# Batch 1 back on TensorE transposes, later work on the DMA crossbar, and new scheduler durations: one change to a fused attention and maxout kernel

## Chip, cores, metric

One core of one Trainium2 chip. The metric is device time in microseconds (us) of one execution. A kernel is timed several times; medians are quoted, over all runs. Ratios are of fast runs alone (here: a run is slow when it is over 1.5% above the fastest of the same kernel). Each run also has a mean granted TensorE clock. Within a call of experiments all kernels run on the same chip, beside runs of the kernel before.

## The reference

Attention over 4 batches, 8 heads, 768 positions, head size 64, with a full causal mask for some heads and "first 4 keys plus a window of 64" for the others, then a feed-forward layer:

```python
scores = scale * np.matmul(q, k.transpose(0, 1, 3, 2))      # masked, softmax over keys
attn   = np.matmul(a, v)                                     # 4 x 8 x 768 x 64
x      = attn.transpose(0, 2, 1, 3).reshape(3072, 512)
out    = np.maximum(x @ w1, x @ w2) @ w_out                  # w1, w2: 512x1024, w_out: 1024x512
```

The kernel uses max(a, b) = b + relu(a - b): out = x (w2 w_out) + relu(x (w1 - w2)) w_out. So it prepares `wd = w1 - w2` and `wm = w2 w_out` once. "Dense work" below means the products with `wd`, `wm` and `w_out`.

## The kernel before

The program is not a loop nest. It is a list of operations with durations, dependences and priorities; a list scheduler in the kernel file runs through them once, at build, on a model clock, and emits each in the order in which the model started it. Each engine, and the SP queue that issues DMAs, then keeps that fixed order on the chip, waiting wherever the chip is later than the model was: in the timeline that the prediction shows, TensorE stands 2.44 us before a score matmul with dense matmuls next in its list.

```python
FIRST_QK_DMA = 4      # from this pair of heads on: q, k narrow and by crossbar
FIRST_X_DMA = 8       # from this pair on: attention output by crossbar
LAT = {"PE": 0.25, "DVE": 0.15, "ACT": 0.2, "POOL": 0.2, "DMA": 1.8}
...
# load of q, k or v of pair i (two heads of one batch, 384 KB of float32)
ld_ops[tag, i] = P.add({"DMA": 1.15 if wide else 1.75}, fn, ...)
...
# q and k of a pair, after the cast to bf16: crossbar ...
if i >= FIRST_QK_DMA:
    tops.append(P.add({"DMA": 0.9}, move, deps=[casts[which]], ...))      # dma_start_transpose
    continue
# ... or six TensorE transposes into PSUM and an eviction
t = P.add({"PE": 0.34}, tr, ...)
tops.append(P.add({"DVE": 1.02, "ACT": 1.02}, evac, deps=[t], ...))       # (cut)
# the scores of a pair depend on both
op = P.add({"PE": cost}, go, deps=tops, row=True, prio=(0, i, bt[0]), ...)
...
if FIRST_X_DMA <= i < len(pairs) - 1:
    xt_ops[b, hp] = P.add({"DMA": 0.9}, xmove, deps=norms, ...)           # crossbar
else:
    t = P.add({"PE": 0.34}, xtr, ...)                                     # TensorE
...
# dense work: four matmuls a piece, lower priority than attention
t = P.add({"PE": PIECE * GT / 2400.0 + 0.005}, up, deps=... wd_ops + [xt_ops[b, hp] ...], prio=(4, b, g, 0, f))
...
P.add({"DMA": 0.8}, store, deps=[e], ...)
```

There are 16 pairs; pairs 4 to 7 are batch 1. All DMAs of q, k, v, weights, output and all crossbar transposes go through the SP queue, in order.

Terms: the crossbar is the DMA path that transposes on the way (`dma_start_transpose`). A wide load of q or k fetches rows of 512 B, a narrow one of 256 B. An eviction is the copy of a result out of PSUM. qt, kt and xt are the transposed q, k and attention output; a wait on kt is TensorE standing before a score matmul until the transposed k has landed. A block is six TensorE transposes. Half clock means a granted TensorE clock of about 0.50.

The softmax here doesn't subtract the row's maximum and nothing guards it: scores larger than these inputs give would overflow.

Of the kernel before, what the change touches and what calls it, by code (L numbers as in the profile page):

```python
# [13 lines left out]
NEG = -30000.0  # L14
ACT_SLACK = 0.6
PIECE = 4
FIRST_QK_DMA = 4
FIRST_X_DMA = 8


SWITCH = 0.1
# [112 lines left out]
def kernel(  # L134
# [13 lines left out]
    nc = tc.nc  # L148
# [9 lines left out]
    d_model = H * D  # L158
    d_ff = moe_w1.shape[1]
    KC = d_model // 128  # L160
    FC = d_ff // 128
    HP = H // 2
# [15 lines left out]
    w1_f = consts.tile([128, KC, d_ff], F32)  # L178
    w2_f = consts.tile([128, KC, d_ff], F32)
# [25 lines left out]
    P = Planner(res)  # L205
# [69 lines left out]
    def plan_load(i, b, hp, which):  # L275
        src = (q, k, v)[which][b, 2 * hp:2 * hp + 2]
        tag = ("ldq", "ldk", "ldv")[which]
        wide = which < 2 and i < FIRST_QK_DMA
        pat = ("h (m p r) d -> p h m (r d)", dict(p=128, r=2)) if wide else ("h (n p) d -> p h n d", dict(p=128))

        def fn(eng):
            dst = P[tag, i]
            if which < 2 and not wide:
                dst = dst.rearrange("p h m (r d) -> p h (m r) d", d=D)
            nc.sync.dma_start(out=dst, in_=src.rearrange(pat[0], **pat[1]))  # L285
        ld_ops[tag, i] = P.add({"DMA": 1.15 if wide else 1.75}, fn, acq=[(tag, (tag, i))], prio=(len(ld_ops),))

    def plan_weight(name, arr, dst, parts):
        src = arr.rearrange("(c p) f -> p c f", p=128)
        w = src.shape[1] // parts  # L290
        for i in range(parts):
            def fn(eng, i=i):
                nc.sync.dma_start(out=dst[:, i * w:(i + 1) * w, :], in_=src[:, i * w:(i + 1) * w, :])
            ld_ops[name, i] = P.add({"DMA": 6.0 / parts}, fn, prio=(len(ld_ops),))


    xt_ops = {}
# [3 lines left out]
    def plan_pair(i, b, hp):  # L301
# [15 lines left out]
        for which in range(2):  # L317
            tb, tt = (("qb", "qt"), ("kb", "kt"))[which]

            if i >= FIRST_QK_DMA:  # L320
                def move(eng, tb=tb, tt=tt):
                    nc.sync.dma_start_transpose(
                        out=P[tt, i].rearrange("p (n c) -> p n c", c=128),
                        in_=P[tb, i].rearrange("p n h d -> p (n h d)"))
                tops.append(P.add({"DMA": 0.9}, move, deps=[casts[which]], acq=[(tt, (tt, i))], rel=[(tb, i)],
                                  prio=(0, i, which)))
                continue

            def tr(eng, which=which, tb=tb):
                src = P[tb, i]  # L330
                o = P["mmT", i, which].bitcast(BF16)
                for n in range(NB):
                    nc.tensor.transpose(o[:, n * 128:(n + 1) * 128], src[:, n].rearrange("p h d -> p (h d)"), ident)

            def evac(eng, which=which, tt=tt):
                o, in_ = P[tt, i], P["mmT", i, which].bitcast(BF16)[:, 0:S]
                if i < FIRST_QK_DMA:
                    o = o.rearrange("q (m p r) -> q m r p", p=128, r=2)
                    in_ = in_.rearrange("q (m r p) -> q m r p", p=128, r=2)
                ev(eng)(out=o, in_=in_)  # L340
            t = P.add({"PE": 0.34}, tr, deps=[casts[which], ident_op], acq=[("mm", ("mmT", i, which)), (tt, (tt, i))],
                      rel=[(tb, i)], prio=(1, i, which))
            tops.append(P.add({"DVE": 0.56, "ACT": 0.72} if i >= FIRST_QK_DMA else {"DVE": 1.02, "ACT": 1.02}, evac, deps=[t],
                              rel=[("mmT", i, which)], prio=(1, i, which)))
# [111 lines left out]
                out=P["xt", b][:, hp, :].rearrange("p (n c) -> p n c", c=128),  # L456
                in_=P["x", i].rearrange("p n c -> p (n c)"))
        if FIRST_X_DMA <= i < len(pairs) - 1:
            xt_ops[b, hp] = P.add({"DMA": 0.9}, xmove, deps=norms, prio=(0, i, NS),
                                  use=[("x", ("x", i), 3), ("xt", ("xt", b), XT_USES)])  # L460
        else:
            t = P.add({"PE": 0.34}, xtr, deps=norms, acq=[("mm", ("mmX", i))], prio=(2, i, NS),
                      use=[("x", ("x", i), 3), ("xt", ("xt", b), XT_USES)])
            xt_ops[b, hp] = P.add({"DVE": 0.56, "ACT": 0.72}, xev, deps=[t], rel=[("mmX", i)], prio=(0, i, NS))
# [4 lines left out]
    def plan_weights_prep():  # L469
        w2_ops = []  # L470
        for c in range(KC):
            w2_ops.append(P.add({"POOL": 1.15, "ACT": 0.95, "DVE": 0.75}, copy(w2_bf[:, c, :], w2_f[:, c, :]),
                                deps=[ld_ops["w2", c // 2]], prio=(3, 0, c)))
        for c in range(0, FC, 2):
            wo_ops.append(P.add({"POOL": 1.15, "ACT": 0.95, "DVE": 0.75}, copy(wo_bf[:, c:c + 2, :], wo_f[:, c:c + 2, :]),
                                deps=[ld_ops["wo", c // 4]], prio=(3, 1, c)))
        for c in range(KC):
            def fn(eng, c=c):
                nc.vector.tensor_sub(out=wd_bf[:, c, :], in0=w1_f[:, c, :], in1=w2_bf[:, c, :])
            wd_ops.append(P.add({"DVE": 1.15}, fn, deps=[ld_ops["w1", c // 2], w2_ops[c]], prio=(3, 2, c)))  # L480
        t_ops = []
        for f in range(FC):
            def tr(eng, f=f):
                psb = P["mmW", f].bitcast(BF16)
                for c in range(KC):
                    nc.tensor.transpose(psb[:, c * 128:(c + 1) * 128], w2_bf[:, c, f * 128:(f + 1) * 128], ident)

            def evac(eng, f=f):
                ev(eng)(out=w2t[:, f, :], in_=P["mmW", f].bitcast(BF16)[:, 0:d_model])
            t = P.add({"PE": 0.22}, tr, deps=w2_ops, acq=[("mm", ("mmW", f))], prio=(3, 0, f))  # L490
            t_ops.append(P.add({"DVE": 0.42, "ACT": 0.5}, evac, deps=[t], rel=[("mmW", f)], prio=(2, 0, f)))
        for c in range(KC):
            def mm(eng, c=c):
                for f in range(FC):
                    nc.tensor.matmul(P["mmM", c], lhsT=w2t[:, f, c * 128:(c + 1) * 128], rhs=wo_bf[:, f, :],  # L495
                                     start=(f == 0), stop=(f == FC - 1))

            def evac(eng, c=c):
                ev(eng)(out=wm_bf[:, c, :], in_=P["mmM", c])
            t = P.add({"PE": FC * 0.2165}, mm, deps=t_ops + wo_ops, acq=[("mm", ("mmM", c))], prio=(3, 1, c))  # L500
            wm_ops.append(P.add({"DVE": 0.6, "ACT": 0.6}, evac, deps=[t], rel=[("mmM", c)], prio=(2, 1, c)))


    def plan_dense(b):
        mm = "mm" if b < B - 1 else "sc"
        prev = [None]
        for g in range(NG):
            ups = []
            for f in range(FC):
                t = None  # L510
                for part in range(KC // PIECE):
                    def up(eng, g=g, f=f, part=part):
                        for c in range(part * PIECE, (part + 1) * PIECE):
                            nc.tensor.matmul(P["mmH", b, g, f][:, 0:GT], lhsT=wd_bf[:, c, f * 128:(f + 1) * 128],  # L514
                                             rhs=P["xt", b][:, c, g * GT:(g + 1) * GT],
                                             start=(c == 0), stop=(c == KC - 1))
                    t = P.add({"PE": PIECE * GT / 2400.0 + 0.005}, up,
                              deps=[t] if part else wd_ops + [xt_ops[b, hp] for hp in range(HP)] + [prev[0]],
                              acq=[] if part else [(mm, ("mmH", b, g, f))],
                              use=[("xt", ("xt", b), XT_USES)] + ([] if part else [("gt", ("gt", b, g), GT_USES)]),  # L520
                              prio=(3, b, g, 0, f) if part else (4, b, g, 0, f))
# [10 lines left out]
            for t in range(GT // 128):  # L532
# [22 lines left out]
                def store(eng, g=g, t=t, c0=c0):  # L555
# [1 line left out]
                    nc.sync.dma_start(out=out[r0:r0 + 128, :], in_=P["ot", b, g, t])  # L557
                e = P.add({"ACT": 0.6, "DVE": 0.6}, evac, deps=[last], acq=[("ot", ("ot", b, g, t))],
                          rel=[("mmY", b, g, t)], prio=(0, 0, 9))
                P.add({"DMA": 0.8}, store, deps=[e], rel=[("ot", b, g, t)], prio=(0, 0, 9))  # L560

    pairs = [(b, hp) for b in range(B) for hp in range(HP)]

# [2 lines left out]
    with tc.manual_schedule():  # L566
# [3 lines left out]
        for h in range(H):  # L570
            def fn(eng, h=h):
                nc.vector.tensor_scalar(out=msk[:, h], in0=code, scalar1=thr[:, h:h + 1], scalar2=None, op0=ALU.is_ge)
            mask_ops.append(P.add({"DVE": 0.35}, fn, prio=(1, h // 2, 3)))
        for i in (0, 1):
            for w in range(3):
                plan_load(i, *pairs[i], w)
        plan_weight("w2", moe_w2, w2_f, 2)
        for i in (2, 3):
            for w in range(3):
                plan_load(i, *pairs[i], w)  # L580
        plan_weight("wo", moe_w_out, wo_f, 2)
        plan_weight("w1", moe_w1, w1_f, 2)
        for i in range(HP, len(pairs)):
            for w in range(3):
                plan_load(i, *pairs[i], w)
# [46 lines left out]
```

## Time and profile before

| | before |
|---|---|
| timed runs | 213.3 us median (211.2 to 215.2) |
| span of the profiled run | 208.5 us |
| TensorE busy / idle in the span | 183.5 / 25.0 us |
| of the idle: first 47 us / 47 to 150 us | 13.9 / 7.2 us |
| waits of the scores for k, after 47 us | 7.0 us in 6 waits |
| DMA packets | 98,916 |

Read it from TensorE: idle time at the start is in good part the fill of the pipeline (the longest wait, 6.9 us, is for the first q); idle time later is what better order could remove. The lines are in the prediction.

### The profile page before, as it was taken

To read this page: it belongs to the slowest core of one execution; us is meant where nothing else is said; L and a number is where in the kernel's file an instruction comes from. 1 tells how busy PE (TensorE), PEld (TensorE's weight loads), DVE (VectorE), ACT (ScalarE), POOL (GpSimd) and SP (SyncE) were. 2 spreads that over 40 slices of the span, in tenths; PEclk is the share of its full clock that TensorE was granted. 3 is DMA by queue.
4 is the path that set the end of the run, shared out by engine and by line. 5 is a ranking of instruction groups with operands and counts; after the bars stand their busy time and mean duration, and the time that the engine had idled before them with its cause. 6 is when DMAs were issued, how large, how long until landed. Compare 5 with 4: busy or idle time off the path is not lost.

```text
span 208.5 us, 4406 instructions
## 1 busy us (share of the span) xinstructions
PE 183.5 (88%) x1702; PEld 95.2 (46%) x1702; DVE 119.5 (57%) x273; ACT 124.0 (59%) x240; POOL 47.6 (23%) x59
## 2 busy tenths in 40 slices
PE   0388886999999799959997999979999999999992
PEld 0244553544554356523463545534454465444540
DVE  7799989957796477614574357427454084030700
ACT  2489699724888788947866795959692200212021
POOL 0155547053333132331231332314000000000000
PEclk9999999999999999988999999999999999999999
DMA  4999999969999999999999999999630210212112
GB/s 117 268 344 323 258 350 410 250 129 220 236 174 240 176 246 218 173 195 191 233 175 207 229 251 205 228 171 252 156 27 15 89 50 0 101 53 101 50 50 101
DMA packets 98916, 37.84 MB, mean 181 GB/s; under 512 B 87632, under 2 KB 93776, under 8 KB 98896
## 3 DMA queue, kind: packets, MB, share of 16 engines
q1 hardware_dynamic: 98752, 37.56, 87.1%
q8 instruction: 13, 0.21, 0.5%
q14 instruction: 7, 0.06, 0.1%
q10 hardware_dynamic: 144, 0.01, 0.0%
HBM read 25.17 MB, written 6.29 MB: 151 GB/s over the span
## 4 chain that ended last, share of the span: by engine, by line
PE 42%; DMA 26%; DVE 13%; SPq 6%; ACT 5%; issue 3%; POOL 2%; POOLq 0%; ACTq 0%; DVEq 0%
PE bank_80 L543 8%; DMA vn_87<-in_v_dram 6%; DMA kn_86<-in_k_dram 6%; SPq L285 4%; PE bank_79 L543 4%; PE bank_79 L514 4%; DMA kt_100<-kb_93 3%; PE bank_80 L514 3%; DMA kn_84<-in_k_dram 3%; DMA vn_89<-in_v_dram 3%; PE bank_80 L495 3%; DMA out_dram<-ot_125 3%; PE bank_74 L543 2%; PE bank_73 L543 2%; DMA kn_85<-in_k_dram 2%
## 5 line engine op out<-in xcount | busy, mean ns | idle before, releaser
L514 PEld LDWEIGHTS <-wd_bf 128*128 128x128 bf16 x256 | 23.0, 98 | 16.6 <-issue 3.0
L368 ACT ACTIVATE at_101<-bank_73 128x512 bf16<-128x512 f32 x16 | 9.6, 597 | 12.4 <-PE bank_74 L356 12.4
L379 DVE TENSOR_TENSOR at_101<-at_101,msk 128x512 bf16<-128x512 bf16 x16 | 8.0, 500 | 12.0 <-ACT at_101 L368 12.0
L356 PE MATMUL bank_73<-qt_98,kt_100 64*128 64x256 bf16 (+1 forms) x48 | 9.2, 271 | 5.9 <-DMA kt_100<-kb_93 5.9
L356 PEld LDWEIGHTS <-kt_100 64*128 64x128 bf16 x160 | 5.6, 94 | 17.1 <-issue 8.5
L543 PEld LDWEIGHTS <-gt_124 128*128 128x128 bf16 x96 | 8.9, 100 | 9.9 <-issue 1.4
L543 PEld LDWEIGHTS <-gt_123 128*128 128x128 bf16 x96 | 8.6, 98 | 9.8 <-issue 0.8
L379 DVE TENSOR_TENSOR at_109<-at_109,msk 128x384 bf16<-128x384 bf16 x16 | 7.9, 493 | 8.9 <-ACT at_109 L368 8.8
L368 ACT ACTIVATE at_107<-bank_75,bias_j 128x512 bf16<-128x512 f32 x16 | 11.1, 695 | 2.4 <-PE bank_76 L356 2.3
L356 PEld LDWEIGHTS <-kt_99 64*128 64x128 bf16 x160 | 5.5, 95 | 13.2 <-issue 8.7
L368 ACT ACTIVATE at_103<-bank_75,bias_64 128x512 bf16<-128x512 f32 x16 | 11.1, 692 | 0.6 <-PE bank_76 L356 0.6
L356 PE MATMUL bank_73<-qt_97,kt_99 64*128 64x256 bf16 (+1 forms) x48 | 9.5, 276 | 2.2 <-DVE kt_99 L340 1.1
L527 DVE TENSOR_SCALAR gt_124<-bank_80 128x384 bf16<-128x384 f32 x9 | 5.0, 558 | 10.8 <-ACT ot_127 L553 5.8
L368 ACT ACTIVATE at_104<-bank_76,bias_64 128x512 bf16<-128x512 f32 x16 | 11.1, 696 | 0.0
L368 ACT ACTIVATE at_108<-bank_76,bias_j 128x512 bf16<-128x512 f32 x16 | 11.1, 691 | 0.0
L368 ACT ACTIVATE at_111<-bank_75,bias_j 128x256 bf16<-128x256 f32 x16 | 7.7, 480 | 5.2 <-PE bank_76 L356 5.2
L368 ACT ACTIVATE at_105<-bank_73 128x512 bf16<-128x512 f32 x16 | 9.8, 613 | 1.6 <-PE bank_74 L356 1.6
L543 PE MATMUL bank_79<-wo_bf,gt_124 128*128 128x512 bf16 x40 | 10.1, 379 | 0.0
L553 ACT COPY ot_125<-bank_80 128x512 f32<-128x512 f32 x3 | 1.8, 585 | 14.0 <-PE bank_80 L543 14.0
L379 DVE TENSOR_TENSOR at_105<-at_105,msk 128x512 bf16<-128x512 bf16 x16 | 8.0, 502 | 3.6 <-ACT at_105 L368 3.6
L543 PE MATMUL bank_80<-wo_bf,gt_123 128*128 128x512 bf16 x40 | 10.0, 380 | 0.0
L368 ACT ACTIVATE at_106<-bank_74 128x512 bf16<-128x512 f32 x16 | 9.9, 621 | 0.0
(225 smaller groups left out, 494.8 us busy)
## 6 DMA issues: line engine op xcount, KB each, us to landing
w_f<-in_moe_w_dram SPq DMA_DIRECT2D x4, 1024.0 KB, 9.2
qn_81<-in_q_dram SPq DMA_DIRECT2D x6, 384.0 KB, 4.7
kn_84<-in_k_dram SPq DMA_DIRECT2D x6, 384.0 KB, 5.6
vn_87<-in_v_dram SPq DMA_DIRECT2D x6, 384.0 KB, 6.5
wo_f<-in_moe_w_out_dram SPq DMA_DIRECT2D x2, 1024.0 KB, 8.2
out_dram<-ot_125 SPq DMA_DIRECT2D x8, 256.0 KB, 2.3
out_dram<-ot_126 SPq DMA_DIRECT2D x8, 256.0 KB, 2.4
out_dram<-ot_127 SPq DMA_DIRECT2D x8, 256.0 KB, 2.4
```

Of the source, the lines that this page charges most:

```text
L285: nc.sync.dma_start(out=dst, in_=src.rearrange(pat[0], **pat[1]))
L356: nc.tensor.matmul(P["sc", i, st, hh][:, off:off + w], lhsT=kt[64 * hh:64 * hh + 64, j * 128:(j + 1) * 128], rhs=qt[64 * hh:64 * hh + 64, ...
L368: nc.scalar.activation(out=P["at", i, st, hh][:, 0:n], in_=P["sc", i, st, hh][:, 0:n], func=ACT.Exp, scale=scale, bias=bias)
L379: nc.vector.tensor_mul(out=at[:, 0:n], in0=at[:, 0:n], in1=mk)
L495: nc.tensor.matmul(P["mmM", c], lhsT=w2t[:, f, c * 128:(c + 1) * 128], rhs=wo_bf[:, f, :], start=(f == 0), stop=(f == FC - 1))
L514: nc.tensor.matmul(P["mmH", b, g, f][:, 0:GT], lhsT=wd_bf[:, c, f * 128:(f + 1) * 128], rhs=P["xt", b][:, c, g * GT:(g + 1) * GT], start=( ...
L527: nc.vector.tensor_relu(out=o, in_=i_)
L543: nc.tensor.matmul(ps, lhsT=lhsT, rhs=rhs, start=(i == 0), stop=(i == KC + FC - 1))
L553: ev(eng)(out=P["ot", b, g, t], in_=P["mmY", b, g, t])
```

## The change

Its intent: batch 1 keeps wide loads and TensorE transposes for q, k; the crossbar serves q, k of batches 2 and 3 and the attention output from batch 1; w1 comes in column halves, so that dense work can start on half of it. Beside that, the scheduler's durations for DMAs are changed, and the weight product is cut in pairs of matmuls. Core of the diff:

```diff
-FIRST_QK_DMA = 4
-FIRST_X_DMA = 8
+FIRST_QK_DMA = 8
+FIRST_X_DMA = 4
-        ld_ops[tag, i] = P.add({"DMA": 1.15 if wide else 1.75}, fn, ...)
+        ld_ops[tag, i] = P.add({"DMA": 1.15 if wide else 1.85}, fn, ...)
-                tops.append(P.add({"DMA": 0.9}, move, ...))
+                tops.append(P.add({"DMA": 1.35}, move, ...))
-                    o = o.rearrange("q (m p r) -> q m r p", p=128, r=2)
-                    in_ = in_.rearrange("q (m r p) -> q m r p", p=128, r=2)
+                    o = o.rearrange("q (m p r) -> q m p r", p=128, r=2)
+                    in_ = in_.rearrange("q (m r p) -> q m p r", p=128, r=2)
-            xt_ops[b, hp] = P.add({"DMA": 0.9}, xmove, ...)
+            xt_ops[b, hp] = P.add({"DMA": 1.35}, xmove, ...)
-                P.add({"DMA": 0.8}, store, ...)
+                P.add({"DMA": 0.75}, store, ...)
 # (cut) weights: w1 loaded in column halves, wd = w1 - w2 in eight halves of high priority
-            wd_ops.append(P.add({"DVE": 1.15}, fn, deps=[ld_ops["w1", c // 2], w2_ops[c]], prio=(3, 2, c)))
+                wd_ops.append(P.add({"DVE": 0.6}, fn, deps=[ld_ops["w1", c, half * FC // 2], w2_ops[c]],
+                                    prio=(0.5, 2, c)))
-            t = P.add({"PE": FC * 0.2165}, mm, deps=t_ops + wo_ops, acq=[("mm", ("mmM", c))], prio=(3, 1, c))
+            for f0 in range(0, FC, 2):          # (cut) two matmuls a piece
+                t = P.add({"PE": 2 * 0.2165}, mm, ..., prio=(5, 0, c) if f0 == 0 else (3.5, 0, c))
-                              deps=[t] if part else wd_ops + [xt_ops[b, hp] for hp in range(HP)] + [prev[0]],
+                              deps=[t] if part else wd_ops[KC * (f // (FC // 2)):][:KC] + [xt_ops[b, hp] for hp in range(HP)] + [prev[0]],
```

More of the change, by code (lines that the diff above doesn't have):

```diff
@@ L285, in fn, with plan_weight @@
             nc.sync.dma_start(out=dst, in_=src.rearrange(pat[0], **pat[1]))
-        ld_ops[tag, i] = P.add({"DMA": 1.15 if wide else 1.75}, fn, acq=[(tag, (tag, i))], prio=(len(ld_ops),))
-    def plan_weight(name, arr, dst, parts):
-        src = arr.rearrange("(c p) f -> p c f", p=128)
-        w = src.shape[1] // parts
-        for i in range(parts):
-            def fn(eng, i=i):
-                nc.sync.dma_start(out=dst[:, i * w:(i + 1) * w, :], in_=src[:, i * w:(i + 1) * w, :])
-            ld_ops[name, i] = P.add({"DMA": 6.0 / parts}, fn, prio=(len(ld_ops),))
+        ld_ops[tag, i] = P.add({"DMA": 1.15 if wide else 1.85}, fn, acq=[(tag, (tag, i))], prio=(len(ld_ops),))
+    def plan_weight(name, arr, dst, rows, cols):
+        src = arr.rearrange("(c p) f -> p c f", p=128)[:, rows, cols]
+        mb = 512e-6 * (rows.stop - rows.start) * (cols.stop - cols.start)
+        def fn(eng):
+            nc.sync.dma_start(out=dst[:, rows, cols], in_=src)
+        op = P.add({"DMA": mb * 2.8}, fn, prio=(len(ld_ops),))
+        for c in range(rows.start, rows.stop):
+            for f in range(cols.start // 128, cols.stop // 128):
+                ld_ops[name, c, f] = op
     xt_ops = {}
@@ L324, in move @@
                         in_=P[tb, i].rearrange("p n h d -> p (n h d)"))
-                tops.append(P.add({"DMA": 0.9}, move, deps=[casts[which]], acq=[(tt, (tt, i))], rel=[(tb, i)],
+                tops.append(P.add({"DMA": 1.35}, move, deps=[casts[which]], acq=[(tt, (tt, i))], rel=[(tb, i)],
                                   prio=(0, i, which)))
@@ L458, in plan_pair @@
         if FIRST_X_DMA <= i < len(pairs) - 1:
-            xt_ops[b, hp] = P.add({"DMA": 0.9}, xmove, deps=norms, prio=(0, i, NS),
+            xt_ops[b, hp] = P.add({"DMA": 1.35}, xmove, deps=norms, prio=(0, i, NS),
                                   use=[("x", ("x", i), 3), ("xt", ("xt", b), XT_USES)])
@@ L472, in plan_weights_prep, with fn @@
             w2_ops.append(P.add({"POOL": 1.15, "ACT": 0.95, "DVE": 0.75}, copy(w2_bf[:, c, :], w2_f[:, c, :]),
-                                deps=[ld_ops["w2", c // 2]], prio=(3, 0, c)))
+                                deps=[ld_ops["w2", c, f] for f in range(FC)], prio=(3, 0, c)))
         for c in range(0, FC, 2):
             wo_ops.append(P.add({"POOL": 1.15, "ACT": 0.95, "DVE": 0.75}, copy(wo_bf[:, c:c + 2, :], wo_f[:, c:c + 2, :]),
-                                deps=[ld_ops["wo", c // 4]], prio=(3, 1, c)))
-        for c in range(KC):
-            def fn(eng, c=c):
-                nc.vector.tensor_sub(out=wd_bf[:, c, :], in0=w1_f[:, c, :], in1=w2_bf[:, c, :])
-            wd_ops.append(P.add({"DVE": 1.15}, fn, deps=[ld_ops["w1", c // 2], w2_ops[c]], prio=(3, 2, c)))
+                                deps=[ld_ops["wo", c_, f] for c_ in (c, c + 1) for f in range(KC)], prio=(3, 1, c)))
+        for half in range(2):
+            fs = slice(half * d_ff // 2, (half + 1) * d_ff // 2)
+            for c in range(KC):
+                def fn(eng, c=c, fs=fs):
+                    nc.vector.tensor_sub(out=wd_bf[:, c, fs], in0=w1_f[:, c, fs], in1=w2_bf[:, c, fs])
+                wd_ops.append(P.add({"DVE": 0.6}, fn, deps=[ld_ops["w1", c, half * FC // 2], w2_ops[c]],
+                                    prio=(0.5, 2, c)))
         t_ops = []
@@ L492, in plan_weights_prep, with mm @@
         for c in range(KC):
-            def mm(eng, c=c):
-                for f in range(FC):
-                    nc.tensor.matmul(P["mmM", c], lhsT=w2t[:, f, c * 128:(c + 1) * 128], rhs=wo_bf[:, f, :],
-                                     start=(f == 0), stop=(f == FC - 1))
+            t = None
+            for f0 in range(0, FC, 2):
+                def mm(eng, c=c, f0=f0):
+                    for f in range(f0, f0 + 2):
+                        nc.tensor.matmul(P["mmM", c], lhsT=w2t[:, f, c * 128:(c + 1) * 128], rhs=wo_bf[:, f, :],
+                                         start=(f == 0), stop=(f == FC - 1))
+                t = P.add({"PE": 2 * 0.2165}, mm, deps=[t] + (t_ops + wo_ops if not f0 else []),
+                          acq=[] if f0 else [("mm", ("mmM", c))], prio=(5, 0, c) if f0 == 0 else (3.5, 0, c))
             def evac(eng, c=c):
                 ev(eng)(out=wm_bf[:, c, :], in_=P["mmM", c])
-            t = P.add({"PE": FC * 0.2165}, mm, deps=t_ops + wo_ops, acq=[("mm", ("mmM", c))], prio=(3, 1, c))
             wm_ops.append(P.add({"DVE": 0.6, "ACT": 0.6}, evac, deps=[t], rel=[("mmM", c)], prio=(2, 1, c)))
@@ L559, in plan_dense @@
                           rel=[("mmY", b, g, t)], prio=(0, 0, 9))
-                P.add({"DMA": 0.8}, store, deps=[e], rel=[("ot", b, g, t)], prio=(0, 0, 9))
+                P.add({"DMA": 0.75}, store, deps=[e], rel=[("ot", b, g, t)], prio=(0, 0, 9))
     pairs = [(b, hp) for b in range(B) for hp in range(HP)]
@@ L573 @@
             mask_ops.append(P.add({"DVE": 0.35}, fn, prio=(1, h // 2, 3)))
-        for i in (0, 1):
-            for w in range(3):
-                plan_load(i, *pairs[i], w)
-        plan_weight("w2", moe_w2, w2_f, 2)
-        for i in (2, 3):
-            for w in range(3):
-                plan_load(i, *pairs[i], w)
-        plan_weight("wo", moe_w_out, wo_f, 2)
-        plan_weight("w1", moe_w1, w1_f, 2)
+        ORDER = ("p0", "p1", "w2", "p2", "p3", "wo", "w1")
+        for what in ORDER:
+            if what[0] == "p":
+                for w in range(3):
+                    plan_load(int(what[1:]), *pairs[int(what[1:])], w)
+            elif what == "w2":
+                for c in (0, 2):
+                    plan_weight("w2", moe_w2, w2_f, slice(c, c + 2), slice(0, d_ff))
+            elif what == "wo":
+                for c in (0, 4):
+                    plan_weight("wo", moe_w_out, wo_f, slice(c, c + 4), slice(0, d_model))
+            else:
+                for half in (0, 1):
+                    plan_weight("w1", moe_w1, w1_f, slice(0, KC), slice(half * d_ff // 2, (half + 1) * d_ff // 2))
         for i in range(HP, len(pairs)):
```

## The prediction

> **What bounds the kernel now.** I read the page first (engine shares and the 40 slices), then busy time by stretches, then TensorE's waits after 47 us, then the order of time around its longest wait, then the groups of the lines that the change touches.
>
> ```profile
> PE 183.5 (88%) x1702; PEld 95.2 (46%) x1702; DVE 119.5 (57%) x273; ACT 124.0 (59%) x240; POOL 47.6 (23%) x59
> PE   0388886999999799959997999979999999999992
> PEclk9999999999999999988999999999999999999999
> DMA  4999999969999999999999999999630210212112
> ```
>
> TensorE (PE) is the busiest engine. Its row shows two regions: the first ten slices (to about 50 us) with holes, and then nearly solid 9s to the end with four thin slices (7, 5, 7, 7). The DMA row is full until about 150 us and then nearly empty. So two things could set the end: TensorE work, or the DMA stream that feeds attention until 150 us. Busy time by stretches (columns: stretch, its length, then busy us and instruction counts of PE, PEld, DVE, ACT, POOL, the granted clock, DMA share, GB/s):
>
> ```profile
> 38.00:47.00 9.00, 8.55 (x69) 4.23 (x66) 6.35 (x11) 4.19 (x9) 3.29 (x3) 1.00 0.89 168
> 47.00:60.00 13.00, 12.87 (x118) 6.25 (x117) 9.72 (x19) 9.68 (x20) 4.14 (x5) 1.00 1.36 213
> 60.00:75.00 15.00, 13.53 (x160) 6.97 (x158) 8.58 (x20) 11.53 (x24) 3.82 (x5) 1.00 1.15 206
> 75.00:82.00 7.00, 7.00 (x84) 3.90 (x82) 6.21 (x15) 5.97 (x13) 2.06 (x3) 1.00 1.10 235
> 82.00:105.00 23.00, 20.56 (x202) 9.45 (x200) 11.36 (x31) 17.27 (x34) 6.82 (x8) 0.93 1.26 202
> 105.00:150.00 45.00, 41.88 (x436) 21.38 (x433) 23.98 (x58) 33.38 (x68) 11.57 (x13) 1.00 1.19 210
> 150.00:205.00 55.00, 54.52 (x330) 27.81 (x328) 19.26 (x39) 13.21 (x27) 0.00 (x0) 1.00 0.18 58
> ```
>
> From 47 us (the first dense matmul of batch 0 is at 46.8) to 205 us TensorE is busy 150.4 of 158 us: 7.6 us idle. The dense matmuls fill whatever attention leaves, so from there on **the end is the sum of TensorE's work plus its idle time**. A DMA stage that merely finishes sooner gains nothing by itself; it only moves dense work from before to after. The idle time is nearly all of one kind:
>
> ```profile
> PE bank_73 L356 <- DMA kt_100<-kb_93: 5.9, 5, 2.4
> PE bank_73 L356 <- DMA kt_99<-kb_92: 1.1, 1, 1.1
> PE bank_80 L543 <- ACT ot_125 L553: 0.3, 1, 0.3
> ```
>
> L356 is the score matmul; six times it was placed in TensorE's fixed order ahead of dense work and then waited for a k block still in the crossbar: 7.0 us. The longest wait costs twice:
>
> ```profile
> 88.45 0.26 PE L417 MATMUL bank_77<-vb_96,at_109 128*128 128x65 bf16 x3
> ...
> 91.25 0.28 PE L356 MATMUL bank_73<-qt_98,kt_100 64*128 64x256 bf16 x1 [2.44 <-DMA kt_100<-kb_93]
> ...
> 91.57 1.04 PE L543 MATMUL bank_80<-wm_bf,xt_120 128*128 128x512 bf16 x4
> ...
> 93.29 1.90 PE L543 MATMUL bank_80<-wo_bf,gt_124 128*128 128x512 bf16 x4
> ```
>
> After 2.4 us of idle, four matmuls that took 1.04 us take 1.90: the clock by single microseconds is 0.75, 0.50, 0.50, 0.54 from 92 to 96 us. The lost clock is 0.25+0.50+0.50+0.46 = 1.7 us. So what better waiting could win is 7.0 + 1.7 = 8.7 us, beside what the first 47 us may give.
>
> **What the Trainium skill says.** (1) "TensorE: Matmul & The Clock Gate", section Why this matters for your kernels, asks for no idle gaps of more than about 3 us between bursts, else the clock halves. The trace agrees in kind, and shows it already after a 2.4 us wait. (2) "Advanced Engine Details and Errata", section X-Bar Transpose (TRN2), says that transpose DMAs are as fast as regular ones. The trace: a crossbar transpose of 196 KB (128x768 bf16) lands 4.0 us after issue (median), a plain 384 KB load of q or k 4.3 to 5.6 us; so per byte it is slower here[...]. (3) "DMA: Bandwidth & Descriptors", Specifications, puts full rate at transfers of 512 B and more. Here narrow q, k rows are 256 B and wide ones 512 B; the stretch 60 to 108 us, nearly all packets below 512 B, moves 208 GB/s, the stretch 20 to 36 us, with weights, 332. Agrees in direction. (4) "VectorE: DVE Perf Modes", section What auto-detection actually checks, gives the packed 16-bit mode only with step 1 on every tensor. The trace agrees: eviction L453 with contiguous tensors takes 0.55 us, L340, which writes with a step of two, 1.02 us for the same 768 elements.
>
> ```profile
> L322 SPq DMA_TRANSPOSE kt_100<-kb_93 x6: 1237/1282/1669, 51.9 to 145.3; - x6
> L340 DVE COPY kt_100<-bank_80 x2: 1019/1021/1023, 14.2 to 29.7; 128x768 bf16<-128x768 bf16 x2
> L453 DVE COPY xt_121<-bank_80 x2: 557/558/559, 69.0 to 84.9; 128x768 bf16<-128x768 bf16 x2
> ```
>
> (Columns: duration ns min, median, max; first and last start.)
>
> **The change part by part.**
> *Batch 1 (pairs 4 to 7), TensorE.* q, k go back to TensorE: 8 blocks of six transposes. Six take 0.50 us as shown (L449) but the next matmul issues 0.34 us after the first, so 8 x 0.34 = 2.7 us added. The attention output of the four pairs leaves TensorE: 4 x 0.34 = 1.4 us removed. Net **+1.3 us on the path**, as TensorE is the bound there.
> *Evictions.* 8 x 1.02 us come to VectorE or ScalarE and 4 x 0.56 to 0.80 go. The new order reads with a step of 128 elements and writes contiguously: still not step 1 everywhere, so I expect about 1.0 us again. Between 47 and 82 us VectorE is busy 24.5 of 35 us, ScalarE 27.2; 6 us more over the two fit. Off the path, **0**.
> *DMA.* By packets: a narrow q, k or v load is 1536 of 256 B, a wide one 768 of 512 B, a transpose 768. A pair of batch 1 had 3 x 1536 + 2 x 768 = 6144, and gets 2 x 768 + 1536 + 768 = 3840. At 34.0 thousand packets per 48 us (60 to 108 us), 1.41 ns each, that is 8.7 against 5.4 us, as an estimate: some **13 us of DMA less over the batch** (less if 512 B packets take longer). Batches 2 and 3 keep 6912 packets a pair, 9.8 us. So the loads end near 138 us rather than 150, but by the argument above this is worth only the waits that it removes. The wait in batch 1 (1.4 us at pair 7) should go; the waits of batches 2 and 3, 5.6 us, remain possible, since a pair's k still goes through the crossbar.
> *The order.* All engine orders are fixed at build by a list scheduler. It held a transpose for 0.9 us of DMA; the issue alone takes 1.2 to 1.3 us. With 1.35, 1.85 for a narrow load and 0.75 for a store it places the scores later, behind dense pieces. I expect this, with the head start, to leave about 2.5 of the 7.0 us of waits, so **-4.5 us**, and no gap long enough for the clock to fall, most likely: **-1.2 us** (0.7 of 1.7).
> *The weights.* w1 in column halves with early differences lets the first dense matmuls start after half of them; the combined weight product (L495, 4 runs of 8 matmuls of 1.7 to 1.9 us) is cut in pairs that attention can pass. Now the blocks delay pair 3: its last probabilities are masked at 40.0 us and its output product ends at 42.5. But TensorE is busy 8.55 of 9 us from 38 to 47, and the first 37 us are filled by VectorE (7.93 of 8 us from 30 to 38) and by loads in unchanged order. At most **-1 us; I take -0.7**. Pair 4 starts some 4 us sooner than 49.2 us, as two crossbar trips of 4 us go; this moves work, not the sum.
> Sum: +1.3 - 4.5 - 1.2 - 0.7 = -5.1 us, from a median of 213.1 gives 208.0.
>
> **Rivals.** (a) *The DMA is the real bound.* For: the chain of waits runs through loads and crossbar trips from 62 to 150 us, and DMA share is above 1. Then 13 us less DMA would show up nearly whole: about 201. Against: only 7.6 us of TensorE is idle after 47 us, so it cannot give more than about 9. (b) *A new wait for the old.* The two banks that dense work and transposes share are now held 8 times for 0.34 + 1.02 us and semaphore time, and the in-order SP queue now holds x transposes in batch 1 ahead of later loads; if TensorE waits 0.5 us at each of the 8 that is 4 us back, and with the 1.3 us the gain is gone: 212 to 213. For: the L340 evictions already hold TensorE 1.1 us at 9 us. Against: at 50 to 82 us the order has attention and dense pieces to put between. (c) *Waits of batches 2 and 3 stay whole*: only the batch 1 wait (1.4) and 0.7 go, +1.3 paid: about 212.
>
> **Range and chances.** The three timed runs span 211.2 to 213.5, so the time itself is loose by 1 us. My step of largest doubt is how many of the 7.0 + 1.7 us stay: all gone and a better start gives 204, none gone 213. Range 203.5 to 212.5. The limit for faster by over 2% is 4.3 us, just under the sum of 5.1; I give that 0.56, within 2% 0.40, slower 0.04.
>
> **What would show it.** Packets near 90.2 thousand rather than 98.9 (98.9 - 12.3 - 3.1 + 6.1 + 0.5). TensorE's work (busy less waits) about 1.3 us more; waits on kt after 47 us at 1 to 4 us; no half clock after 50 us; DMA full only until about 140 us; first L514 at 45 to 47 us; evictions L340-like at 1.0 us. I am wrong if the gain is over 9 us (then the early stretch or the dense rate changed), if waits for evictions take the place of those on the crossbar, or if kt waits stay near 7 us.

## The result, and the profile after

| | before | after |
|---|---|---|
| timed runs | 213.29 us median (4 runs) | 204.99 us median (203.62 to 206.59, 4 runs) |
| ratio of fast runs | | 0.9646 (95% interval 0.9534 to 0.9758) |
| span of the profiled run | 208.5 | 201.7 |
| TensorE busy / idle | 183.5 / 25.0 | 184.9 / 16.8 |
| idle: first 47 us / 47 to 150 us | 13.9 / 7.2 | 12.3 / 0.8 |
| waits of scores for k after 47 us | 7.0 | 0.4 |
| DMA packets | 98,916 | 90,084 |

A ratio is the mean time of one kernel's fast runs over that of the other's fast runs of the same rounds, so not quite the ratio of the medians.

Line numbers moved with the edit: scores are L360 (L356 before), the output product L421 (L417), dense L524 and L553 (L514 and L543), q and k evictions L344 (L340), crossbar of q, k L326 (L322). From the page of the kernel after, engine shares and three rows of the 40 slices:

```profile
PE 184.9 (92%) x1726; PEld 96.7 (48%) x1726; DVE 121.2 (60%) x281; ACT 123.6 (61%) x240; POOL 47.6 (24%) x59
PE   0399988889999999999999999999999999999992
PEclk9999999999999999999999999999999999999999
DMA  3999999999999999999998989998621200212112
```

TensorE's thin slices after the first ten are gone, and so are the two 8s of the clock. The DMA row is full to about 141 us (28 slices of 5.04 us); before it was full to 146 us (28 of 5.21). Busy time by stretches after (same columns as in the prediction):

```profile
47.00:60.00 13.00, 12.77 (x155) 7.29 (x154) 12.03 (x24) 11.78 (x23) 6.65 (x8) 1.00 1.20 244
60.00:75.00 15.00, 15.00 (x165) 7.00 (x161) 10.59 (x25) 13.04 (x26) 5.47 (x6) 1.00 1.23 206
75.00:82.00 7.00, 7.00 (x97) 3.89 (x94) 4.32 (x12) 6.85 (x15) 0.87 (x1) 1.00 0.95 158
82.00:105.00 23.00, 22.44 (x234) 11.17 (x230) 12.65 (x32) 18.38 (x39) 4.34 (x6) 1.00 1.24 198
105.00:150.00 45.00, 45.00 (x422) 22.81 (x419) 24.07 (x57) 31.66 (x64) 9.85 (x12) 1.00 0.93 189
```

The second figure of each row reaches the length of the stretch: 102.2 of the 103 us from 47 to 150 are busy, 95.8 before. TensorE's waits after 47 us (engine, line, releaser: total us, times, longest), in full:

```profile
PE bank L337 <- DVE qt L344: 0.6, 2, 0.4
PE bank L360 <- DMA kt<-kb: 0.4, 1, 0.4
```

The kt waits, 7.0 us before, are 0.4 us. And the instructions whose cost the change could alter (duration ns min, median, max; first and last start):

```profile
L344 DVE COPY kt<-bank x5: 945/957/958, 9.4 to 55.3; 128x768 bf16<-128x768 bf16 x5
L344 ACT COPY kt<-bank x3: 798/798/798, 24.6 to 64.3; 128x768 bf16<-128x768 bf16 x3
L326 SPq DMA_TRANSPOSE kt<-kb x8: 1210/1238/2128, 70.6 to 142.5; - x8
```

Where did the 6.8 us of span come from? TensorE's idle time fell by 8.2 us (25.0 to 16.8) and its busy time rose by 1.4, though the half clock that had stretched it by 1.7 us is gone. That is bookkeeping; it does not yet say which part of the change removed the waits. Two theories:

- **A: the order.** The scheduler believed in crossbar transposes of 0.9 us and so put scores ahead of dense work before k could be there. Longer durations put dense work first, and the waits go. Moving batch 1 off the crossbar then only adds TensorE work.
- **B: the relief.** The DMA stream was too full for q and k to arrive in time; taking 8,800 packets away lets them arrive. The durations are cosmetics.

### The profile page after: what moved, and what is told of

It is laid out like the page before. It is cut to its first block, busy times and chain, and to the rows that moved or that the text cites. A ratio compares the mean times of both kernels' runs of the same rounds, so it can differ in the third digit from the quotient of the medians.

```text
span 201.7 us, 4459 instructions
## 1 busy us (share of the span) xinstructions
PE 184.9 (92%) x1726; PEld 96.7 (48%) x1726; DVE 121.2 (60%) x281; ACT 123.6 (61%) x240; POOL 47.6 (24%) x59
## 2 busy tenths in 40 slices
DMA packets 90084, 37.05 MB, mean 184 GB/s; under 512 B 72144, under 2 KB 84432, under 8 KB 90064
## 4 chain that ended last, share of the span: by engine, by line
PE 73%; DMA 15%; DVE 3%; ACT 3%; issue 2%; POOL 1%; SPq 1%; ACTq 0%; POOLq 0%; DVEq 0%
PE bank L553 30%; PE bank L524 20%; PE bank L360 10%; PE bank L421 10%; DMA qn<-in_q_dram 7%; DMA kn<-in_k_dram 3%; DMA vn<-in_v_dram 3%; PE bank L337 2%; DMA kt<-kb 2%; ACT at L372 2%; POOL qb L311 1%; DVE qt L344 1%; DVE at L383 1%; PE bank L504 1%; DVE msk L582 1%
## 5 line engine op out<-in xcount | busy, mean ns | idle before, releaser
L383 DVE TENSOR_TENSOR at<-at,msk 128x512 bf16<-128x512 bf16 (+1 forms) x96 | 42.4, 465 | 20.1 <-ACT at L372 19.3
L372 ACT ACTIVATE at<-bank 128x512 bf16<-128x512 f32 (+1 forms) x96 | 49.3, 573 | 8.0 <-PE bank L360 7.7
L553 PE MATMUL bank<-wo_bf,gt 128*128 128x512 bf16 x192 | 47.2, 379 | 0.0
L524 PE MATMUL bank<-xt,wd_bf 128*128 128x384 bf16 x256 | 46.9, 326 | 0.0
L537 DVE TENSOR_SCALAR gt<-bank 128x384 bf16<-128x384 f32 x49 | 27.2, 557 | 30.5 <-PE bank L524 28.6
L372 ACT ACTIVATE at<-bank,bias_j 128x512 bf16<-128x512 f32 (+1 forms) x64 | 33.9, 586 | 6.2 <-PE bank L360 6.0
L360 PE MATMUL bank<-qt,kt 64*128 64x256 bf16 (+3 forms) x320 | 35.8, 293 | 1.6 <-DVE kt L344 1.1
L421 PE MATMUL bank<-vb,at 128*128 128x65 bf16 x672 | 35.1, 197 | 1.3 <-DVE at L383 0.8
L421 PEld LDWEIGHTS <-at 128*128 128x128 bf16 x672 | 27.0, 99 | 15.4 <-issue 6.4
L524 PEld LDWEIGHTS <-wd_bf 128*128 128x128 bf16 x256 | 23.1, 98 | 16.2 <-issue 2.5
L553 PEld LDWEIGHTS <-gt 128*128 128x128 bf16 x192 | 17.3, 98 | 19.0 <-issue 1.4
L553 PE MATMUL bank<-wm_bf,xt 128*128 128x512 bf16 x96 | 24.7, 379 | 0.0
L360 PEld LDWEIGHTS <-kt 64*128 64x128 bf16 x320 | 11.1, 95 | 24.1 <-issue 19.1
L311 POOL CAST kb<-kn 128x768 bf16<-128x768 f32 x15 | 12.9, 857 | 20.0 <-DMA kn<-in_k_dram 18.9
L553 PEld LDWEIGHTS <-xt 128*128 128x128 bf16 x96 | 8.6, 98 | 9.0 <-issue 0.6
L337 PE MATMUL bank<-ident,qb 128*128 128x128 bf16 x48 | 4.7, 242 | 7.5 <-ACT qb L311 7.2
```

The costliest lines, as they stand in the source:

```text
L311: ev(eng)(out=dst.rearrange("p n h d -> p h n d"), in_=src.rearrange("p h m (r d) -> p h (m r) d", d=D))
L337: nc.tensor.transpose(o[:, n * 128:(n + 1) * 128], src[:, n].rearrange("p h d -> p (h d)"), ident)
L360: nc.tensor.matmul(P["sc", i, st, hh][:, off:off + w], lhsT=kt[64 * hh:64 * hh + 64, j * 128:(j + 1) * 128], rhs=qt[64 * hh:64 * hh + 64, ...
L372: nc.scalar.activation(out=P["at", i, st, hh][:, 0:n], in_=P["sc", i, st, hh][:, 0:n], func=ACT.Exp, scale=scale, bias=bias)
L383: nc.vector.tensor_mul(out=at[:, 0:n], in0=at[:, 0:n], in1=mk)
L421: nc.tensor.matmul(po[:, qb_ * (D + 1):(qb_ + 1) * (D + 1)], lhsT=at[:, off + t * 128:off + (t + 1) * 128], rhs=vb[:, hh, j, :], start=(st ...
```

## The experiments

Twelve kernels in three calls; all gave correct results. Names with "before" edit the kernel before, names with "after" the changed one.

### One by one: durations alone, relief alone

```diff
 e1: before, three durations only
-{"DMA": 1.15 if wide else 1.75}   -{"DMA": 0.9} (twice)   -{"DMA": 0.8}
+{"DMA": 1.15 if wide else 1.85}   +{"DMA": 1.35}          +{"DMA": 0.75}
```

> The kernel before with only the scheduler's DMA durations changed (narrow load 1.75 to 1.85, crossbar 0.9 to 1.35, store 0.8 to 0.75); the same loads, transposes and engines. Theory A (the order was wrong: it put scores ahead of dense work before k was there): TensorE's waits on kt after 47 us fall from 7.0 us to 2 or less, no half clock, the time falls 5 to 7 us, to about 207. Theory B (the DMA work itself held things up and had to be taken away): waits on kt stay at 5 us or more, the time within 1.5 us of before.

Measured: 202.5 us median, ratio 0.9639 (0.9577 to 0.9702). With no load, transpose or engine changed, the packets are the same 98,916. Waits of TensorE on kt after 47 us, from its waits:

```profile
PE bank L356 <- DMA kt<-kb: 1.5, 2, 1.1
```

Theory A's waits, and slightly more gain than it asked for. The "no half clock" holds after 47 us only: this profile has one at 37 to 40 us. Theory B is refuted as the main cause: no packet was taken away. And k does not come sooner: the last of the twelve k transposes is issued at 156.7 us against 145.3 before, but 348 dense matmuls have started by then against 264. That is theory A seen in the order itself. One thing moves along: the SP queue's own order changes too, and the same packets are spread thinner (DMA share 1.08 from 47 to 150 us against 1.22). The runs do not separate the two orders.

```diff
 e2: before
-FIRST_QK_DMA = 4
+FIRST_QK_DMA = 8
```

> The kernel before with only q, k of batch 1 loaded wide and transposed on TensorE; durations in the scheduler as before. Theory A: the waits of batches 2 and 3 (5.6 us and the half clock) stay, batch 1's 1.4 us goes, 2.7 us of TensorE work comes: within 2 us of before. Theory B: with some 16 us of DMA gone the waits go nearly whole: waits under 1.5 us, time about 4 to 5 us less.

Measured: 209.3 us, ratio 0.9975 (0.9897 to 1.0053): no gain to be seen. Packets fell to 86,373, fewer than in the change itself. TensorE's waits on kt:

```profile
PE bank L356 <- DMA kt<-kb: 2.8, 2, 2.1
```

The waits did fall, from 7.0 to 2.8 us, more than A expected (5.6) and less than B (under 1.5). But TensorE's busy time in the span is 189.6 us against 183.5: eight blocks of transposes more (4.4 us at the 0.55 us a block found below), and two stretches of half clock (0.66 from 35 to 40 and from 120 to 125 us, 3.4 us lost, against the 1.7 us of before), ate it. So relief alone does shorten the waits; what it saves is spent again on TensorE work.

```diff
 e3: after, the three durations put back
-{"DMA": 1.15 if wide else 1.85}   -{"DMA": 1.35} (twice)   -{"DMA": 0.75}
+{"DMA": 1.15 if wide else 1.75}   +{"DMA": 0.9}            +{"DMA": 0.8}
```

> The changed kernel with the scheduler's old DMA durations; same work. Theory A: waits on kt come back, 3 to 6 us, time 208 to 211. Theory B: waits stay under 1 us, time within 1.5 us of the changed kernel's 205.

Measured: 211.4 us, ratio 1.0042 (0.9972 to 1.0111): with the old durations the whole change is worth nothing. Its waits, and its stretches around the longest of them:

```profile
PE bank L360 <- DMA kt<-kb: 5.8, 5, 2.6
```

```profile
91.00:94.00 3.00, 0.38 (x9) 0.20 (x7) 0.44 (x2) 0.22 (x1) 0.83 (x1) 0.83 0.69 148
94.00:97.00 3.00, 3.00 (x27) 1.55 (x24) 1.28 (x4) 2.35 (x4) 0.83 (x1) 0.50 1.29 247
97.00:100.00 3.00, 3.00 (x11) 0.57 (x8) 1.73 (x5) 1.09 (x2) 0.83 (x1) 0.53 1.37 192
```

The same picture as before: TensorE nearly idle from 91 to 94 us, and then a clock (third figure from the end) of 0.50 and 0.53 for six microseconds. Theory A; the time is just above the 208 to 211 that it gave.

```diff
 e4: before, with the three new durations, FIRST_QK_DMA = 8, FIRST_X_DMA = 4 and the new eviction order; weights as before
```

> All of the change but its weight part (w1 in row halves, whole differences of late priority, weight product in runs of eight matmuls, as before). By my prediction that part is worth 0.7 us: 205.5 to 206. A rival (the early stretch, where TensorE's idle time fell from 14.0 to 12.5 us in the first 50 us, is this part's doing): 206.5 to 208.

Measured: 205.4 us, ratio 0.9771 (0.9716 to 0.9826). This is at the value of my prediction (205.5), but the changed kernel itself measured 204.99 and 204.36. The weight part is worth between nothing and about 1 us; these runs do not resolve it. The run tells something else, though: e4 is e1 plus the batch 1 part, and it is 2.8 us slower (205.4 against 202.6, means of six fast runs), with TensorE busy 186.1 against 183.4 us.

### The four arrangements of batch 1

The next call has the changed kernel as its own control and differs only in who transposes batch 1.

```diff
 e5: after, unedited          (FIRST_QK_DMA = 8, FIRST_X_DMA = 4)
 e6: after, FIRST_QK_DMA = 4, FIRST_X_DMA = 8      # batch 1 as before
 e7: after, FIRST_QK_DMA = 4                       # all of batch 1 by crossbar
 e8: after, FIRST_X_DMA = 8                        # all of batch 1 on TensorE
```

> The changed kernel unedited, as the control of this call: 204 to 206, ratio near 0.965.

> The changed kernel with batch 1 put back as before (q, k narrow and by crossbar, output by TensorE): the new durations and the weight part stay. Theory A (the durations did it, TensorE's work bounds): 1.3 us of TensorE work goes, waits on kt stay at 1 to 2 us, so 203 to 205, not slower than the control. Theory B (batch 1's relief of the DMA matters): waits on kt above 4 us, 208 or more.

> The changed kernel with q, k of batch 1 narrow and by crossbar, its output by crossbar too: the least TensorE work of the four arrangements (2.7 us below the control), the most DMA. If only TensorE's work counts: 202 to 203. If DMA binds with this much of it (10.7 us of scheduled DMA a pair from pair 4 on): the order puts dense work later and TensorE runs out of it or waits, 207 or more. I expect the second.

> The changed kernel with the output of batch 1 transposed on TensorE as before, q, k of batch 1 on TensorE as changed: the most TensorE work (1.4 us above the control), the least DMA. Theory A: waits near 0 as in the control, so control + 1 to 2 us, 206 to 207. A rival (banks shared with dense work are held for 12 more blocks): control + 3 or more.

| | q, k of batch 1 | output of batch 1 | median us | ratio to before | TensorE busy | kt waits after 47 us |
|---|---|---|---|---|---|---|
| e6 | crossbar | TensorE | 202.14 | 0.9645 (0.9542 to 0.9748) | 182.5 | 0.3 |
| e5 (the change) | TensorE | crossbar | 204.36 | 0.9752 (0.9634 to 0.9871) | 184.0 | 0.8 |
| e8 | TensorE | TensorE | 206.78 | 0.9856 (0.9751 to 0.9961) | 186.6 | 0.7 |
| e7 | crossbar | crossbar | 208.12 | 0.9902 (0.9762 to 1.0042) | 184.7 | 3.0 |

The intervals are wide because only two runs of before counted as fast here; the four versions are best compared with each other, by the means of their six fast runs (202.37, 204.44, 206.80; five for e7, 207.76). e6 came out below the 203 to 205 expected, with less wait than the 1 to 2 us. e6 to e5 to e8 is a ladder: each rung adds four blocks of six TensorE transposes net, and costs 2.1 and 2.4 us, while the kt waits stay below 1 us. The page rows of its ends (the changed kernel's is above; x counts matmuls):

```profile
PE 182.5 (91%) x1702; PEld 94.6 (47%) x1702; DVE 124.0 (62%) x280; ACT 122.5 (61%) x237; POOL 46.8 (23%) x59
PE 186.6 (91%) x1750; PEld 97.9 (48%) x1750; DVE 127.5 (62%) x286; ACT 124.7 (61%) x239; POOL 48.6 (24%) x59
```

**With the new durations in place, the part that names the change makes the kernel 2.1 us slower than it need be**, 2.8 us by e1 and e4. A block costs 0.52 to 0.59 us of total time on the ladder; I had counted 0.34. Not all of that is TensorE's work: busy time grows by 1.5 and 2.6 us (two profiles of the changed kernel itself differ by 0.9), and TensorE's idle time in the first 47 us by 0.8 and 1.2 us. Part of that idle time can be seen. The first k and q blocks of batch 1 make TensorE wait, in the changed kernel:

```profile
43.54 0.51 PE L337 MATMUL bank<-ident,qb 128*128 128x128 bf16 x6 [0.34 <-POOL qb L311]
45.17 0.49 PE L337 MATMUL bank<-ident,kb 128*128 128x128 bf16 x6 [0.38 <-DVE qt L344]
49.49 0.49 PE L337 MATMUL bank<-ident,kb 128*128 128x128 bf16 x6 [0.23 <-DVE qt L344]
```

One wait is for the cast of q, two are for the eviction of the q block just before; e5 and e8 have the same three (0.33 and 0.57 us for the first). For e8 the rival (banks shared with dense work) gave control + 3 us or more and theory A + 1 to 2; it measured + 2.4, between the two. After 47 us e8 waits only 0.2 us for such evictions.

e7 is the other side. It has the fewest transposes on TensorE and the most DMA (102,628 packets), and it loses. Its waits after 47 us:

```profile
PE bank L360 <- DMA kt<-kb: 3.0, 2, 1.7
PE bank L360 <- ACT at L372: 1.4, 4, 0.5
PE bank L453 <- DVE x L443: 0.7, 1, 0.7
```

Its clock falls too (0.81 from 92 to 100 us, 0.83 from 130 to 140), which lengthens TensorE's busy time: 184.7 us with 24 matmuls fewer than e6. So with this much DMA the gain is mostly lost. That the DMA stream itself binds here, as theory B would have it, is not shown: its q and k transposes land sooner than e6's (medians 3.0 against 3.3 us after issue), and the DMA share from 105 to 150 us is 1.06 against 1.15. An order that the scheduler built badly for so much scheduled DMA would look the same, and no run separates the two.

### Which duration, how exact, and a faster version

```diff
 e9:  before, only {"DMA": 0.9} to {"DMA": 1.35} (both crossbar places)
 e10: as e1, but the crossbar at 1.1
 e11: as e1, but the crossbar at 1.6
 e12: after, FIRST_QK_DMA = 5, FIRST_X_DMA = 6
```

> The kernel before with one duration changed in the scheduler: crossbar 0.9 to 1.35; load and store durations old. Theory A with the crossbar as the wrong duration: waits on kt at most 2 us, 202 to 205, as with all three durations (202.5). Rival C (the load duration did it, 48 loads by 0.1): waits stay above 4 us, 208 or more.

Measured: 205.2 us, ratio 0.9666 (0.9576 to 0.9756). The profiled run fell in the slow state (mean clock 0.967, with half clock between about 20 and 45 us), so I take only its waits on kt: 0.8 us. One number in the scheduler gives most of the gain. Whether the load duration adds the rest cannot be said from this: the four fast runs spread from 202.8 to 205.5. (Rival C speaks of 48 loads; 40 of them are narrow and carry that duration.)

> The kernel before with new load and store durations and the crossbar at 1.1, about half way. Theory A: between the two ends, waits on kt 2 to 5 us, 204 to 208. Rival D (any other order would have been better than that of before, it was an unlucky one): as good as with 1.35, 201.5 to 203.5, waits near 1 us.

Measured: 203.7 us, ratio 0.9658 (0.9592 to 0.9724), kt waits:

```profile
PE bank L356 <- DMA kt<-kb: 1.1, 2, 0.8
```

My "half way, so half the waits" was wrong: 1.1 does as well as 1.35. Rival D, that any other order would have done, gains by this, but e2 and e3 are two other orders built with 0.9, and both still wait (2.8 and 5.8 us). All four orders built on the kernel before with a longer crossbar (e1, e9, e10, e11) beat it; the two other orders with 0.9 do not (ratios 0.9975 and 1.0042). What the runs support is: too short is bad, and the margin need not be exact. Not tested is which figure of the model was too short: it lets a transpose land 0.9 + 1.8 (`LAT`) = 2.7 us after its start, where the chip took 2.7 to 5.8 us from issue (median 4.0). `LAT` stayed at 1.8 in every run.

> The kernel before with new load and store durations and the crossbar at 1.6, too long. Theory A: no waits on kt in TensorE, but scores are put so late that attention ends late and the dense work runs out ahead of it: TensorE waits on something else late in the kernel, 205 to 210, slower than with 1.35. Rival D: near 202.5.

Measured: 207.4 us, ratio 0.9789 (0.9695 to 0.9882): slower than with 1.1 or 1.35, as A said. Waits after 47 us, the longest:

```profile
PE bank L356 <- DMA kt<-kb: 1.5, 2, 0.9
PE bank L449 <- DVE x L439: 1.2, 1, 1.2
PE bank L356 <- ACT at L368: 0.7, 2, 0.5
PE bank L514 <- DMA xt<-x: 0.5, 1, 0.5
```

Waits on kt did not vanish, against what I wrote; others joined them: attention's own output (x, xt) now comes late for TensorE. Too long a duration moves the idle time to the other side.

> An attempt at a faster version: all of the changed kernel, but q, k by TensorE only up to pair 4 and output by crossbar from pair 6. It has as many transpose blocks on TensorE as batch 1 as before (202.1 us): two more of q, k and two fewer of output. So by TensorE's work alone 202; better than 201.5 only if the head start of pair 4 counts; by the crossing measured with q, k and output of the whole batch on the crossbar (208) nothing is lost as the DMA is not fuller. I expect 201 to 203.

Measured: 202.98 us, ratio 0.9606 (0.9547 to 0.9666), kt waits 0.7 us. As many transpose blocks on TensorE as e6, and the same time within what the two can tell; no gain from the head start of pair 4 shows. So the fastest versions are e6 (202.1), e1 (202.5) and e12 (203.0), against the change's 204.4; only e6 ran beside the change, and I cannot rank the three. They were run at other times.

### The half clock sorts the runs of before

The 26 runs of the kernel before differ by granted clock: the five with a mean clock of 0.997 or more average 209.3 us, the 17 with 0.985 or less 212.6 us, and the four between 212.2. A mean of 0.98 is some 8 us at half clock (0.02 x 209 / 0.5); the profiled run of before, with 0.992, has 3.4 us. So some 3 us of the gap between before and after go with a half clock that most runs of before have: the four runs of the changed kernel with 0.997 or more average 204.3 us, 5.0 below the 209.3. It is also the likely reason why the ratio to before moved between calls (0.9646 and 0.9752 for the same changed kernel): it depends on which runs of before were counted as fast. In before at 92 us and in e3 at 94 us the half clock follows the long wait for k. But it need not be that wait: in the profiles of e9 and e10 it lies early. In e10, a fast run, the clock is 0.50 from 21 us on, and from 11 us to there no wait of TensorE is over 0.5 us; but TensorE is busy only 4.5 of the 6 us before 20 us, and its short waits are for VectorE and ScalarE, not for k. (The changed kernel is busy 6.0 us of that stretch.) The clock row of e10's page:

```profile
PEclk9999699699999999999999999999999999999999
```

Only profiled runs show where the clock fell, so how much of the 3 us is the wait's doing stays open. Of the seven profiles with the old weight part, five (e1, e2, e4, e9, e10) have half clock before 47 us; of the seven with the new one, none. That may be what the weight part is good for; no run was made to test it.

## Why the prediction was right, point by point

The time (208.0, measured 205.0) was within the range; the mechanism, TensorE's waits on the crossbar as the thing to win, was shown. The sizes were not all right, and two errors of opposite sign partly cancelled, the order's gain and batch 1's cost, both set too small:

- **"The end is the sum of TensorE's work plus its idle time."** Shown: e6, e5, e8 move the time by 2.1 and 2.4 us and TensorE's busy time by 1.5 and 2.6 while DMA packets fall from 99,428 to 90,084 to 86,885.
- **"The order ... I expect this, with the head start, to leave about 2.5 of the 7.0 us."** The largest miss: 0.4 us was left, so the term is -6.6, not -4.5. And the head start is not needed: e1 has none and leaves 1.5.
- **"No gap long enough for the clock to fall: -1.2."** The whole 1.7 us went in the profiled pair; between runs of before with and without half clock lie 3.3 us (212.6 against 209.3), not all of it from this wait.
- **"Net +1.3 us on the path" for batch 1.** Sign right, size low: +2.1 us (e5 against e6). The step that failed is pricing a block at its 0.34 us of issue. By the ladder it is 0.52 to 0.59. Waits of 0.34, 0.38 and 0.23 us at the first blocks (0.95 us in all), for a cast and for evictions, are part of the excess; how the rest divides stays open.
- **"The weights: -0.7."** Not resolved; e4 and the changed kernel differ by 0.4 to 1.0 us across calls. TensorE's idle time in the first 47 us did fall by 1.6 us (13.9 to 12.3), but e5, the same kernel, has 12.9, as has e4, without the weight part, and e1, also without it, has 12.1 (e1 and e4 with a clock of 0.96 there, so the busy time is a little stretched). I had said the first dense matmul would start at 45 to 47 us; it starts at 49.8, after the transposes of pairs 4 and 5; and pair 4's scores start at 47.3, 1.9 us sooner than before, not some 4. The kernel still ends earlier, as the sum argument says it may.
- **Sum with measured terms** in the profiled pair: -6.6 - 1.7 + 2.1 and up to -1 for the weights is -6.2 to -7.2; the span fell by 6.8.
- **Rivals.** (a) DMA as the real bound: refuted by e1; what slows e7, with more DMA, is open. (b) a new wait on the shared banks: 0.6 us (L337 waiting for L344), not 4. (c) later waits stay whole: refuted.
- **Signs.** Packets 90.2 thousand foretold (the terms given sum to 90.1), 90.1 measured. Waits on kt 0.4 us, below the 1 to 4 foretold. TensorE's work 1.3 us more foretold; busy time rose by 1.4 although 1.7 us of half clock went, so by 3.1 like for like (2.2 with e5's profile). DMA full until about 140 us: so. Evictions at 1.0 us: VectorE 0.96, but ScalarE 0.80.

## What to carry to other kernels

When instruction order is fixed at build, the durations that the builder believes are part of the kernel: one duration that is too short puts the waiting instruction ahead of work that could have run, and lengthening it, with two small corrections beside it, gained here as much as the whole rewrite that it came with (e1, ratio 0.9639, against 0.9646). So before crediting a change with a gain, run its side edits alone. And where one engine is the bound and filled from a pool of ready work, price a move by what it adds to that engine in total time, not by the issue time of its instructions, and not by what it takes off an engine that has slack.

## What the Trainium skill lacked or had wrong

- "TensorE: Matmul & The Clock Gate", Why this matters for your kernels, asks for gaps below about 3 us. Here a wait of 2.4 us was followed by a clock of 0.50 for about three us (before), one of 2.6 us by 0.50 to 0.53 for six (e3), and in e10 the clock fell to 0.50 at 21 us with no single wait over 0.5 us in the 10 us before. So the length of one gap did not decide it here. It is not the same in each run: 5 of 26 runs of the kernel before had a clock of 0.997 or more.
- "Advanced Engine Details and Errata", X-Bar Transpose (TRN2), calls transpose DMAs as fast as regular ones and gives no issue time (the only table with such counts that I found, in "DMA: Bandwidth & Descriptors", is for trn3 and for earlier generations that it does not name). On the SP queue of the kernel before a transpose of 196 KB took at least 1.21 us to issue, a 384 KB load of q, k or v at least 0.43; the transpose landed 2.7 to 5.8 us after issue, the load 3.5 to 14.9.
- No page gives ScalarE's cost by direction of stride (the nearest, Memory Cachelines in "Advanced Engine Details and Errata", has no duration for it). Its copy of 128x768 from PSUM takes 1.01 us with a write step of two and a contiguous read (L340 before), 0.80 us with a read step of 128 and a contiguous write (L344 after), the same 0.80 as contiguous both ways (L453 before). VectorE goes from 1.02 to 0.96 us by the same edit.
